# Layer-norm statistics of a gMLP gate moved from VectorE to ScalarE and GpSimd, with two changes of buffers beside them

## The chip, the cores and the metric

The kernel runs on one core of a Trainium2 chip. The metric is the time of one execution on the device, in microseconds (us); the lower the better. A core has a matrix engine (TensorE, PE in the profile; PEld is its weight load), VectorE (DVE), ScalarE (ACT), GpSimd (POOL) and SyncE (SP, which only issues transfers). Each runs its own instructions strictly in order and waits on semaphores for the others. TensorE writes to PSUM, eight banks of 128 x 512 floats; the other engines work from SBUF.

## The reference

The input x is 2048 rows of 512. It is normalised per row (xn) and goes two ways: a sliding attention (32 heads of 16, 8 taps two rows apart) with an output projection, and a gated MLP whose gate mixes the rows.

```python
xn = _layernorm(x)
s = attention(xn, wqkv) @ wo
z = gelu(xn @ w_in)                      # 2048 x 1792
z1, z2 = z[..., :896], _layernorm(z[..., 896:])
g = w_sp @ z2 + b_sp[:, None]            # w_sp is 2048 x 2048
return x + s * silu((z1 * g) @ w_out)
```

The change concerns the mean and the variance of `z2`'s rows, 896 values each: `(z - m) / sqrt(v + 1e-5)`.

## The kernel before, in words

All products are done in three passes of single-precision pieces: each operand is split into a high part (a copy on ACT, line 192) and a low part (a subtraction on DVE, line 194), and high x high, high x low and low x high are added in PSUM. So each weight needs one ACT and one DVE instruction before TensorE can use it.

The stages, in the order of TensorE's work:

1. *qkv*: the projections for attention (lines 305 and 382 to 384), until 140.8 us of the profile. Their results go to DRAM.
2. *z1* (lines 676 to 695): seven weights `w1_0` to `w1_6` of 128 columns, for each the four chunks of 512 rows, 12 matmuls a chunk, 10.9 us a weight. Each result is evicted from PSUM with a gelu on ACT (line 692; the first chunk of each weight is first scaled by DVE, line 690) and stored to DRAM.
3. *z2*, the gate (lines 697 to 778): eight pairs of row tiles (i and 8 + i, 128 rows each). Each row tile is computed in two halves of 512 and 384 columns by `z2_half` (lines 705 to 713): 12 matmuls, then a gelu from PSUM into the row tile `zt` (line 713). The weights for the halves are `w2_k_h`, four of each half.
4. *g*, the mixing by `w_sp` (line 802), written as block products over sums and differences of blocks; then the output projections *b* (lines 1044 to 1046, source `ut`) and *s* (the same lines, source the attention's output).

Attention's own arithmetic runs on DVE with low priority throughout (lines 562 to 630): products and reductions of some 2.3 us each, a first addition on POOL (line 617), and an exponential on ACT (line 592), which needs another table than gelu. Its results go through DRAM (`o_d`, line 631) and are needed by *s*.

The loop of stage 3 runs as a pipeline over three turns. In turn i the halves of pair i are computed; the statistics of pair i - 1 are taken (`z2_stats`, line 718); pair i - 2 is normalised (`z2_normal`, line 729) and its blocks combined (`combine`, line 736) and partly stored (`t_d`, lines 750 and 751). In the statistics DVE does two `bn_stats` and one `bn_aggr` a row tile (lines 722 and 723). POOL then makes from mean and variance what the normalisation needs, -m * r and r = (v + eps)^-0.5, each one number a row, in four operations (lines 724 to 727). ACT normalises with these as bias and scale (line 731).

Three sets of buffers matter.

- *Weight slots.* `weight_pair` gives out eight pairs of tiles in turn (`slot`). A weight that takes a slot waits until the last matmul with that slot's former weight. In order of calls they go to 12 weights of qkv, to `w1_0` to `w1_6`, to the four left halves `w2_k_0` and the four right halves `w2_k_1`; so `w2_0_1` to `w2_3_1` take the slots of `w1_3` to `w1_6`. The first weight of stage 4, `wsp_0_0`, has an own pair of tiles with the tags `wh` and `wl` (line 753); a bias (line 954) takes them later. `w_1h` in the profile is the high part of a `w2_k_1`, with numbers left out as in all names; a weight of z1 is `w_0h` to `w_6h` at lines 683 to 685.
- *`t4` tiles*: eight buffers of 128 x 1024, shared by z1's evictions (`z1t`), by the block sums (`sa`, `sb`), by the gate's row tiles `zt` and by a bias that stays for long (`b_a`).
- *PSUM banks*: taken in turn, so that TensorE can be eight halves (two pairs) ahead of ACT's evictions.

`block_sums` (line 388) loads four blocks of `w_sp` (SP), adds them up in four additions (DVE, line 390) and stores the sums to DRAM (POOL, line 400). There are eight such sets for stage 2: set 0 before its first weight, set f + 1 behind weight f.

Instructions are put in order on each engine by a scheduler that works with a model of their times and the priority of program order; a few are pinned to program order (fetches, splits). So a change of a few instructions can move others about. The order is fixed before the kernel runs.

Of the kernel before, what the change touches and what calls it, by code (L numbers as in the profile page):

```python
# [23 lines left out]
KB = D // P  # L24
FB = FH // P
NG = 3
CT = 512
# [17 lines left out]
EPS = 1e-5  # L45
# [12 lines left out]
def kernel(  # L58
# [13 lines left out]
    nc = tc.nc  # L72
# [36 lines left out]
    mone = const.tile([P, 9], F32, name="mone")[:, :1]  # L109
    nc.vector.memset(mone, -1.0)  # L110
    mvx = const.tile([P, NT, 2], F32, name="mvx")
    nc.vector.memset(mvx, 0.0)
    mvz = const.tile([P, NT, 2], F32, name="mvz")
    nmz = const.tile([P, NT], F32, name="nmz")

    BIG = whole.tile([P, NT * 2 * FH + 32], F32R, name="BIG")[:, 32:]
# [6 lines left out]
    def z2_at(j):  # L123
        return planes[:, :, j, 0], planes[:, :, j, 1]
# [19 lines left out]
    def blocks(t, n=KB):  # L144
        return t.rearrange("p (k q) -> p k q", k=n)
# [14 lines left out]
    def weight_pair(name):  # L160
        i = next(slot)
        return (
            wts.tile([P, 512], F32R, tag=f"whi{i}", name=name + "h"),
            wts.tile([P, 512], F32R, tag=f"wlo{i}", name=name + "l"),
        )
# [3 lines left out]
        pin(nc.sync.dma_start(raw[:, :n], src))  # L169
        return raw  # L170

    def prep(src, n, name, raw=None):
        if raw is None:
            raw = fetch(src, n, name)
        hi, lo = weight_pair(name)
        split(hi[:, :n], lo[:, :n], raw[:, :n])
        return hi, lo

# [34 lines left out]
    def late_rstd(j):  # L213
        return mvx[:, j, 1:2] if j < JC else 1.0
# [201 lines left out]
    z1_sums = [(0, i) for i in range(HT)]  # L416
# [254 lines left out]
    def first_sums(a, i):  # L671
        block_sums(a, i, stores=nc.gpsimd)

    first_sums(*z1_sums[0])

    for f in range(FB):
        wh, wl = prep(w_in1[:, f, :], KB * P, f"w1_{f}")
        for c in range(NC):
            pz = mm(f"z1_{f}_{c}")
            for k in range(KB):  # L680
                cc = slice(k * P, (k + 1) * P)
                xh, xl = [planes[:, FB - KB + k, c * JC : (c + 1) * JC, a] for a in range(2)]
# [9 lines left out]
            nc.scalar.activation(zt, pz, AF.Gelu_apprx_tanh)  # L692
# [12 lines left out]
    def z2_half(j, h, zt):  # L705
        xh, xl = xn_at(j)
        pz = mm(f"z2_{j}_{h}")[:, : WID[h]]
        for k in range(KB):
            wh, wl = [w[:, : WID[h]] for w in w2[k, h]]
            nc.tensor.matmul(pz, xh[:, k], wh, start=k == 0, stop=False)  # L710
            nc.tensor.matmul(pz, xh[:, k], wl, start=False, stop=False)  # L711
            nc.tensor.matmul(pz, xl[:, k], wh, start=False, stop=k == KB - 1)  # L712
        nc.scalar.activation(zt[:, HALF[h]], pz, AF.Gelu_apprx_tanh, scale=late_rstd(j))  # L713

    def spatial_block(c, js):
        return prep(w_sp[c, js], CT, f"wsp_{c}_{js}")

    def z2_stats(j, zt):
        st = const.tile([P, 2, 6], F32, tag="st2", name=f"zst_{j}", bufs=3)
        mv, nm = mvz[:, j], nmz[:, j : j + 1]  # L720
        for h in range(2):
            nc.vector.bn_stats(st[:, h], zt[:, h * FQ : (h + 1) * FQ])
        nc.vector.bn_aggr(mv, st)
        nc.gpsimd.tensor_tensor(nm, mv[:, 0:1], mone, op=ALU.mult)
        nc.gpsimd.tensor_scalar(mv[:, 1:2], mv[:, 1:2], EPS, None, op0=ALU.add)
        nc.gpsimd.tensor_tensor(mv[:, 1:2], mv[:, 1:2], nhalf, op=ALU.pow)
        nc.gpsimd.tensor_tensor(nm, nm, mv[:, 1:2], op=ALU.mult)  # L727

    def z2_normal(j, zt, n):
        zh, zl = z2_at(j)  # L730
        nc.scalar.activation(zt, zt, AF.Identity, bias=nmz[:, j : j + 1], scale=mvz[:, j, 1:2])  # L731
# [21 lines left out]
    early_pair = [wts.tile([P, CT], F32R, tag=f"w{n}", name=f"wsp_0_0{n}") for n in "hl"]  # L753
    split(*early_pair, fetch(w_sp[0, 0], CT, "wsp_0_0"))
    spatial = {(0, 0): early_pair}
    b_a = t4("b_a")
# [58 lines left out]
    for n in range(8):  # L815
        a, f = n // 2 % 2, n // 4 * 2 + n % 2
# [333 lines left out]
```

## Time and profile before

| | us |
|---|---|
| median of three runs | 705.97 |
| lowest and highest | 704.80, 706.61 |
| the profiled execution | 707.69 |
| its span, first to last instruction | 705.9 |
| busy in the span: PE, DVE, ACT, POOL | 691.4, 611.1, 280.6, 241.5 |

The profiled execution took 1.8 us more than its span, and 1.7 more than the median of the runs. Times in the profile count from the start of the span. In a row of a timeline stand the start, the duration, engine, line, operation and the tiles written and read; in brackets, where there was any, the time that the engine sat idle before it and what it waited for. In a row of groups, "x16 | 17.9, 1134 | 15.9 <-POOL ..." means sixteen instructions, 17.9 us busy, 1134 ns each, and 15.9 us idle before them, which POOL ended. The granted clock is the share of its full clock that TensorE got.

### The profile page before, as it was taken

How to read it: one execution, taken by the hardware profiler on the slowest of the kernel's cores; microseconds unless marked ns; L12 is line 12 of the kernel's file. 1: busy time of each engine (PE TensorE's matmuls, PEld its weight loads, DVE VectorE, ACT ScalarE, POOL GpSimd, SP SyncE). 2: the span in 40 equal slices, each digit the busy share in tenths (PEclk: the TensorE clock that was granted, in tenths of full speed). 3: DMA queues.
4: the chain of work that ended last, by engine and by line, in shares of the span. 5: the costliest groups of instructions: out<-in, count | busy, mean ns of one | idle time of the engine just before them, and what ended most of it. 6: DMA issues, size and time to landing. Idle time of an engine off the chain costs nothing.

```text
span 705.9 us, 9274 instructions
## 1 busy us (share of the span) xinstructions
PE 691.4 (98%) x3084; PEld 577.3 (82%) x3084; DVE 611.1 (87%) x878; ACT 280.6 (40%) x456; POOL 241.5 (34%) x282
## 2 busy tenths in 40 slices
PE   8999999999997999799999999999999999999997
PEld 7888888888885999688888888888888888888886
DVE  6774387898999999888998999999999999997554
ACT  4343332322424443786443454432443453221530
POOL 3105495932333376632122311223112103541500
PEclk9999999999999899899999999999999999999999
DMA  8769999779999765347799687856848775456894
GB/s 288 242 193 343 328 371 358 241 227 370 350 378 399 297 231 176 120 140 242 240 301 399 201 300 241 265 196 226 278 124 301 252 243 178 127 166 205 262 351 184
DMA packets 102080, 182.37 MB, mean 258 GB/s; under 512 B 9168, under 2 KB 45264, under 8 KB 102032
## 3 DMA queue, kind: packets, MB, share of 16 engines
q1 hardware_dynamic: 56480, 102.14, 43.3%
q0 software_dynamic: 13824, 52.24, 20.7%
q10 hardware_dynamic: 31728, 27.40, 11.6%
q8 instruction: 24, 0.39, 0.2%
q14 instruction: 24, 0.20, 0.1%
HBM read 122.42 MB, written 59.32 MB: 257 GB/s over the span
## 4 chain that ended last, share of the span: by engine, by line
PE 76%; DVE 8%; DMA 7%; issue 4%; POOL 2%; ACT 1%; SPq 1%; DVEq 0%; ACTq 0%; POOLq 0%
PE g L802 39%; PE qkv L382 5%; PE qkv L384 5%; PE qkv L383 5%; DMA sb<-in_w_sp 4%; PE b L1044 4%; PE b L1045 4%; PE b L1046 4%; PE s L1046 2%; PE s L1044 2%; PE s L1045 2%; DVE lg L569 2%; PE qkv L305 1%; DVE pr L562 1%; POOL nmz L727 1%
## 5 line engine op out<-in xcount | busy, mean ns | idle before, releaser
L617 POOL TENSOR_TENSOR pv<-pv 128x1024 f32<-128x1024 f32 x29 | 69.6, 2399 | 78.9 <-DVE pv L606 78.9
L562 DVE TENSOR_TENSOR pr<-k,q 128x2048 f32<-128x2048 f32 x32 | 75.3, 2353 | 8.6 <-DMA k<-qkv_d 4.7
L606 DVE TENSOR_TENSOR pv<-v,lg 128x2048 f32<-128x2048 f32 x32 | 73.3, 2289 | 1.4 <-DMA v<-qkv_d 0.7
L569 DVE TENSOR_REDUCE lg<-pr 128x128 f32<-128x2048 f32 x32 | 73.0, 2280 | 0.1
L631 POOL DMA_DIRECT2D o_d<-tt x32 | 18.1, 565 | 152.4 <-DVE tt L630 152.3
L430 ACT ACTIVATE stage<-qkv 128x512 f32<-128x512 f32 x36 | 21.4, 595 | 50.8 <-PE qkv L384 45.7
L710 PE MATMUL z<-w_0h,BIG 128*128 128x512 f32 x64 | 26.5, 414 | 3.7 <-ACT zt L713 3.7
L622 DVE TENSOR_TENSOR pv<-pv 128x512 f32<-128x512 f32 x32 | 24.0, 750 | 4.4 <-POOL pv L617 4.3
L1055 ACT ACTIVATE bt<-b 128x512 f32<-128x512 f32 x16 | 9.4, 597 | 43.9 <-PE b L1046 43.9
L711 PE MATMUL z<-w_0l,BIG 128*128 128x512 f32 x64 | 26.1, 408 | 0.0
L712 PE MATMUL z<-w_0h,BIG 128*128 128x512 f32 x64 | 26.0, 407 | 0.0
L1099 DVE TENSOR_TENSOR sg<-s,sg 128x512 f32<-128x512 f32 (+1 forms) x17 | 11.2, 659 | 16.9 <-PE s L1046 16.9
L711 PE MATMUL z<-w_1l,BIG 128*128 128x384 f32 x64 | 22.6, 353 | 2.8 <-DVE w_1l L194 2.8
L784 POOL DMA_DIRECT2D ol<-o_d x32 | 17.8, 556 | 20.7 <-DMA o_d<-tt 8.1
L541 POOL DMA_DIRECT2D k<-qkv_d x13 | 7.3, 560 | 50.4 <-DVE pr L562 50.4
L710 PE MATMUL z<-w_1h,BIG 128*128 128x384 f32 x64 | 22.4, 350 | 1.9 <-ACT w_1h L192 1.9
L731 ACT ACTIVATE zt<-zt,nmz,mvz 128x896 f32<-128x896 f32 x16 | 17.9, 1134 | 15.9 <-POOL nmz L727 15.9
L277 DVE TENSOR_TENSOR xT<-xT,mr 128x512 f32<-128x512 f32 x20 | 13.8, 688 | 10.9 <-DMA mr<-mv_d 6.5
L712 PE MATMUL z<-w_1h,BIG 128*128 128x384 f32 x64 | 22.5, 351 | 0.0
L194 DVE TENSOR_TENSOR BIG<-zt,BIG 128x512 fp32r<-128x512 f32 (+2 forms) x24 | 18.4, 771 | 3.7 <-ACT BIG L192 3.7
L802 PE MATMUL g<-ws_3h,BIG 128*128 128x512 f32 x52 | 20.3, 390 | 0.0
L802 PE MATMUL g<-ws_5h,BIG 128*128 128x512 f32 x52 | 20.3, 390 | 0.0
(477 smaller groups left out, 2326.7 us busy)
## 6 DMA issues: line engine op xcount, KB each, us to landing
qkv_d<-stage ACTq DMA_DIRECT2D x24, 512.0 KB
v<-qkv_d POOLq DMA_DIRECT2D x14, 704.0 KB, 4.9
k<-qkv_d POOLq DMA_DIRECT2D x13, 704.0 KB, 6.6
sums_d<-sa POOLq DMA_DIRECT2D x14, 512.0 KB, 6.6
sums_d<-sb POOLq DMA_DIRECT2D x14, 512.0 KB, 9.1
z_d<-z1t ACTq DMA_DIRECT2D x14, 512.0 KB
zl<-z_d SPq DMA_DIRECT2D x12, 512.0 KB
tr<-t_d SPq DMA_DIRECT2D x12, 384.0 KB
```

The source lines that it names most:

```text
L382: nc.tensor.matmul(pq, xh[:, k], wh, start=k == 0, stop=False)
L562: line(nc.vector.tensor_tensor(pr, taps(ks[u], j0), qb.unsqueeze(1).to_broadcast([P, W, NJ * CS]), op=ALU.mult))
L569: line(nc.vector.tensor_reduce(lgs[u][:, :, j0 * HS : (j0 + NJ) * HS], pr.rearrange("p w (i d) -> p w i d", d=DH), axis=AX.X, op=ALU.add,))
L606: line(nc.vector.tensor_tensor(pv.rearrange("p w (i d) -> p w i d", d=DH), taps(vs[u], j0).rearrange("p w (i d) -> p w i d", d=DH), lgs[u] ...
L617: eng.tensor_tensor(pv[:, 0:4], pv[:, 0:4], pv[:, 4:8], op=ALU.add)
L710: nc.tensor.matmul(pz, xh[:, k], wh, start=k == 0, stop=False)
L711: nc.tensor.matmul(pz, xh[:, k], wl, start=False, stop=False)
L712: nc.tensor.matmul(pz, xl[:, k], wh, start=False, stop=k == KB - 1)
L802: nc.tensor.matmul(pg, z[a], w[b], start=start and i == 0, stop=stop and i == 2, skip_group_check=seeded)
L1044: nc.tensor.matmul(pp[:, cols], hi, wh, start=k == 0, stop=False)
L1045: nc.tensor.matmul(pp[:, cols], hi, wl, start=False, stop=False)
L1046: nc.tensor.matmul(pp[:, cols], lo, wh, start=False, stop=k == n - 1)
```

## The change

It has three parts.

1. *Own tiles for the last weight of z1.* `w1_6` no longer takes a slot of the eight; it gets the pair tagged `wh` and `wl`, which `wsp_0_0` takes after it. All later weights move up by one slot.
2. *Two sets of block sums in front of z1*: sets 0 and 7 before the first weight, and nothing behind the last.
3. *The statistics.* Each gelu of the gate also gives the sum of its outputs (`accum_out`), one number a row. POOL makes -mean of the two sums. ACT then squares the row tile with that as bias, writes the squares to where the high part will stand later (they are not used) and gives their sum. POOL makes the variance plus eps, its power and the product. The two `bn_stats` and the `bn_aggr` on DVE go.

```diff
+    def side_pair(name):
+        return [wts.tile([P, CT], F32R, tag=f"w{n}", name=name + n) for n in "hl"]
-    def prep(src, n, name, raw=None):
+    def prep(src, n, name, raw=None, pair_=None):
...
-        hi, lo = weight_pair(name)
+        hi, lo = pair_ or weight_pair(name)
...
     first_sums(*z1_sums[0])
+    first_sums(*z1_sums[FB])
     for f in range(FB):
-        wh, wl = prep(w_in1[:, f, :], KB * P, f"w1_{f}")
+        pair_ = side_pair("w1_last") if f == FB - 1 else None
+        wh, wl = prep(w_in1[:, f, :], KB * P, f"w1_{f}", pair_=pair_)
...
-        first_sums(*z1_sums[f + 1])
+        if f < FB - 1:
+            first_sums(*z1_sums[f + 1])
...
-        nc.scalar.activation(zt[:, HALF[h]], pz, AF.Gelu_apprx_tanh, scale=late_rstd(j))
+        nc.scalar.activation(
+            zt[:, HALF[h]], pz, AF.Gelu_apprx_tanh, scale=late_rstd(j), accum_out=zsum(j, h)
+        )
+    def zsum(j, n):
+        return sums_z[:, 3 * j + n : 3 * j + n + 1]
...
     def z2_stats(j, zt):
-        st = const.tile([P, 2, 6], F32, tag="st2", name=f"zst_{j}", bufs=3)
-        mv, nm = mvz[:, j], nmz[:, j : j + 1]
-        for h in range(2):
-            nc.vector.bn_stats(st[:, h], zt[:, h * FQ : (h + 1) * FQ])
-        nc.vector.bn_aggr(mv, st)
-        nc.gpsimd.tensor_tensor(nm, mv[:, 0:1], mone, op=ALU.mult)
-        nc.gpsimd.tensor_scalar(mv[:, 1:2], mv[:, 1:2], EPS, None, op0=ALU.add)
-        nc.gpsimd.tensor_tensor(mv[:, 1:2], mv[:, 1:2], nhalf, op=ALU.pow)
-        nc.gpsimd.tensor_tensor(nm, nm, mv[:, 1:2], op=ALU.mult)
+        rstd, nm = mvz[:, j : j + 1], nmz[:, j : j + 1]
+        nc.gpsimd.tensor_scalar(
+            nm, zsum(j, 0), zsum(j, 1), -1.0 / FH, op0=ALU.add, op1=ALU.mult
+        )
+        nc.scalar.activation(
+            z2_at(j)[0], blocks(zt, FB), AF.Square, bias=nm, accum_out=zsum(j, 2)
+        )
+        nc.gpsimd.tensor_scalar(rstd, zsum(j, 2), 1.0 / FH, EPS, op0=ALU.mult, op1=ALU.add)
+        nc.gpsimd.tensor_tensor(rstd, rstd, nhalf, op=ALU.pow)
+        nc.gpsimd.tensor_scalar(nm, nm, rstd, None, op0=ALU.mult)
```

Besides, `early_pair` is made by `side_pair`, the constant `mone` goes, `mvz` keeps one number a row tile in place of two, and `sums_z` holds three.

More of the change, by code (lines that the diff above doesn't have):

```diff
@@ L108 @@
     nc.vector.memset(nhalf, -0.5)
-    mone = const.tile([P, 9], F32, name="mone")[:, :1]
-    nc.vector.memset(mone, -1.0)
     mvx = const.tile([P, NT, 2], F32, name="mvx")
     nc.vector.memset(mvx, 0.0)
-    mvz = const.tile([P, NT, 2], F32, name="mvz")
+    mvz = const.tile([P, NT], F32, name="mvz")
+    sums_z = const.tile([P, 3 * NT], F32, name="sums_z")
     nmz = const.tile([P, NT], F32, name="nmz")
@@ L718, in z2_stats @@
     def z2_stats(j, zt):
-        st = const.tile([P, 2, 6], F32, tag="st2", name=f"zst_{j}", bufs=3)
-        mv, nm = mvz[:, j], nmz[:, j : j + 1]
-        for h in range(2):
-            nc.vector.bn_stats(st[:, h], zt[:, h * FQ : (h + 1) * FQ])
-        nc.vector.bn_aggr(mv, st)
-        nc.gpsimd.tensor_tensor(nm, mv[:, 0:1], mone, op=ALU.mult)
-        nc.gpsimd.tensor_scalar(mv[:, 1:2], mv[:, 1:2], EPS, None, op0=ALU.add)
-        nc.gpsimd.tensor_tensor(mv[:, 1:2], mv[:, 1:2], nhalf, op=ALU.pow)
-        nc.gpsimd.tensor_tensor(nm, nm, mv[:, 1:2], op=ALU.mult)
+        rstd, nm = mvz[:, j : j + 1], nmz[:, j : j + 1]
[8 more added lines that the diff above has]
+        nc.gpsimd.tensor_scalar(nm, nm, rstd, None, op0=ALU.mult)
     def z2_normal(j, zt, n):
         zh, zl = z2_at(j)
-        nc.scalar.activation(zt, zt, AF.Identity, bias=nmz[:, j : j + 1], scale=mvz[:, j, 1:2])
+        nc.scalar.activation(zt, zt, AF.Identity, bias=nmz[:, j : j + 1], scale=mvz[:, j : j + 1])
         split(zh[:, :n], zl[:, :n], blocks(zt, FB)[:, :n])
@@ L751, in combine @@
         nc.sync.dma_start(t_d[2, i], b21)
-    early_pair = [wts.tile([P, CT], F32R, tag=f"w{n}", name=f"wsp_0_0{n}") for n in "hl"]
+    early_pair = side_pair("wsp_0_0")
     split(*early_pair, fetch(w_sp[0, 0], CT, "wsp_0_0"))
```

## The prediction

> **What bounds the kernel now.** I read the page's busy shares first, then TensorE's waits, then the stretches around them.
>
> ```profile
> PE 691.4 (98%) x3084; PEld 577.3 (82%) x3084; DVE 611.1 (87%) x878; ACT 280.6 (40%) x456; POOL 241.5 (34%) x282
> ```
>
> TensorE sets the end: whatever doesn't give it back idle time gives nothing. So the next view is who it waited for (total, times, longest, in us):
>
> ```profile
> PE z L710 <- ACT zt L713: 3.7, 1, 3.7
> PE z L711 <- DVE w_1l L194: 2.8, 1, 2.8
> PE z L710 <- ACT w_1h L192: 1.9, 1, 1.9
> ```
>
> All three lie in one stage, the gate's half of the projection (lines 705 to 713). The stretches (length, then PE, PEld, DVE, ACT and POOL busy, granted clock, DMA share, GB/s) show what they cost:
>
> ```profile
> 216.73:222.20 5.47, 5.47 (x26) 4.54 (x25) 5.47 (x5) 3.00 (x6) 2.48 (x2) 1.00 1.04 406
> 222.20:236.00 13.80, 9.12 (x35) 8.12 (x34) 13.60 (x23) 4.43 (x7) 6.16 (x8) 0.75 1.03 396
> 236.00:282.50 46.50, 46.50 (x233) 41.78 (x231) 45.63 (x77) 20.31 (x30) 28.42 (x37) 1.00 0.60 209
> 282.50:295.00 12.50, 8.79 (x27) 6.92 (x27) 10.95 (x24) 8.35 (x15) 6.54 (x13) 0.73 0.36 113
> 295.00:308.60 13.60, 13.60 (x72) 12.62 (x71) 10.59 (x23) 11.22 (x18) 6.09 (x15) 1.00 0.36 134
> 308.60:330.40 21.80, 21.77 (x96) 17.64 (x96) 19.46 (x28) 15.37 (x27) 9.39 (x16) 1.00 0.58 186
> ```
>
> Each stop takes the granted clock down with it (0.75 and 0.73), so its price is idle time plus slow matmuls. TensorE's timeline gives both; the first and last row bound the stage:
>
> ```profile
> 216.95 0.39 PE L710 MATMUL z<-w_0h,BIG 128*128 128x512 f32 x1
> ...
> 223.80 0.34 PE L712 MATMUL z<-w_1h,BIG 128*128 128x384 f32 x1
> ...
> 234.34 0.40 PE L711 MATMUL z<-w_0l,BIG 128*128 128x512 f32 x1
> ...
> 294.75 0.33 PE L710 MATMUL z<-w_1h,BIG 128*128 128x384 f32 x1
> 298.94 0.39 PE L710 MATMUL z<-w_0h,BIG 128*128 128x512 f32 x1
> ...
> 304.42 0.33 PE L710 MATMUL z<-w_1h,BIG 128*128 128x384 f32 x1
> 308.60 0.39 PE L802 MATMUL g<-wsp_0h,BIG 128*128 128x512 f32 x1
> ```
>
> From 298.94 to 308.60 an undisturbed pair of row tiles takes 9.66: 24 matmuls of 512 columns (0.228 apart) and 24 of 384 (0.174 apart). Eight pairs are 77.3; the stage took 308.60 - 216.95 = 91.65, so 14.35 is lost. The first stop: between 223.80 and 234.34 lie 16 steps of 384 and one of 512, worth 3.0, in 10.5: 7.5 lost. The second has the rest, 6.85, of which 3.7 is idle, so some 3 is slow clock. After 308.60 TensorE is full (21.77 of 21.80): what is gained here arrives at the end, if nothing later is late.
>
> **Part 1: own tiles for the last weight.** The 8 weight slots go round. Before, the last right-half weight takes the slot of w1_6, which is read until 216.95:
>
> ```profile
> 225.43 0.52 ACT L192 ACTIVATE w_1h<-w_1r 128x384 fp32r<-128x384 f32 x1
> 228.66 0.55 DVE L194 TENSOR_TENSOR w_1l<-w_1r,w_1h 128x384 fp32r<-128x384 f32 x1
> ```
>
> The high part comes 8.5 after the slot is free, the low part 11.7. After, w1_6 has its own pair, every later weight moves one slot forward, and the last takes the slot of w1_5, free one weight (48 matmuls of 0.227 = 10.9) earlier. With the same lags the low part ends at 228.66 + 0.55 - 10.9 = 218.3; TensorE wants it at 224.0. The stop goes: **-7.5**. The pair is shared with wsp_0_0, whose split now waits for w1_6 to be read out; its reader is L802, from 308.60, which hides that. The fetch and split counts are unchanged.
>
> **Part 2: block sums moved forward.** Set 7 was issued behind the last z1 weight; now it stands before the first. Its two loads on SP, four additions on DVE and two stores on POOL are not removed, they leave this stage:
>
> ```profile
> 258.04 0.64 DVE L390 TENSOR_TENSOR sb<-sa,sb 128x512 f32<-128x512 f32 x1
> L713 ACT ACTIVATE zt<-z,mvx 128x512 f32<-128x512 f32 x4 | 2.7, 683 | 9.5 <-DMA sums_d<-sa 7.2 <-PE z L712 2.3
> ```
>
> The first gate eviction waited 7.2 for a sums store: the sums hold the t4 buffers that the gate's rows need, and set 7 still added at 258. With it gone seven buffers (the bias has one) serve three and a half pairs from the start. In front, set 7 stands where set 1 was, with as many loads and additions, so I take 0. If its four additions (4 x 0.64 = 2.6) came on top before a z1 eviction, and that emptied TensorE's lead, the cost would be up to 2.6 plus the 3 of slow clock; nothing there argues for a gain.
>
> **Part 3: the statistics.** Off DVE go these:
>
> ```profile
> L722 DVE BATCH_NORM_STATS2 zst<-zt 128x6 f32<-128x448 f32 x32 | 18.4, 609 | 0.0
> L723 DVE BATCH_NORM_AGGREGATE mvz<-zst 128x2 f32<-128x12 f32 x16 | 3.0, 192 | 0.0
> ```
>
> 21.4 leaves DVE. To ACT come 16 squares over 128x896 and 48 sums read out (32 evictions, 16 squares). The nearest rows:
>
> ```profile
> L731 ACT ACTIVATE zt<-zt,nmz,mvz 128x896 f32<-128x896 f32 x16 | 17.9, 1134 | 15.9 <-POOL nmz L727 15.9
> L192 ACT ACTIVATE BIG<-zt 128x896 fp32r<-128x896 f32 x8 | 7.6, 948 | 0.1
> L713 ACT ACTIVATE zt<-z 128x512 f32<-128x512 f32 x12 | 7.1, 588 | 0.0
> L713 ACT ACTIVATE zt<-z 128x384 f32<-128x384 f32 x12 | 5.8, 487 | 1.0 <-PE z L712 1.0
> ```
>
> A square has one per-row operand: between the copy without (0.948) and the normalisation with two (1.134), 1.04; x16 = 16.7. No row shows a read-out of the sum: at least 0, at most a whole 384-column activation (0.487, x48 = 23.4). I take the line through 384 and 512 columns at no columns, 0.588 - 4 x 0.101 = 0.18; x48 = 8.6. ACT was busy 3.00 + 4.43 + 20.31 + 8.35 + 11.22 = 47.3 in the stage, so it needs 72.6, against 77.3 for TensorE. ACT's last gate eviction may end some 2.5 after TensorE's stage (an estimate: five evictions of 0.5), so 79.8 - 72.6 = 7.2 of waiting is free. **That is the crux**, because ACT is in order and the normalisation now waits twice for POOL: sum, square, variance, power, product.
>
> ```profile
> L727 POOL TENSOR_TENSOR nmz<-nmz,mvz 128x1 f32<-128x1 f32 x16 | 14.9, 934 | 0.7
> L724 POOL TENSOR_TENSOR nmz<-mvz,mone 128x1 f32<-128x1 f32 x16 | 7.1, 446 | 16.9 <-DVE mvz L723 16.7
> 278.58 5.68 POOL L727 TENSOR_TENSOR nmz<-nmz,mvz 128x1 f32<-128x1 f32 x1
> 284.13 0.19 DVE L723 BATCH_NORM_AGGREGATE mvz<-zst 128x2 f32<-128x12 f32 x1
> 284.29 1.13 ACT L731 ACTIVATE zt<-zt,nmz,mvz 128x896 f32<-128x896 f32 x1 [4.61 <-POOL nmz L727]
> ```
>
> This is the cause of the second stop. A 128x1 product took 5.68 and ended as DVE reached an operation with one tensor input; ACT sat 4.61, the evictions behind it came late, TensorE ran out of banks. POOL in turn idled 16.7 for DVE's statistics, which stand behind attention work. So of ACT's 15.9 I put half, 8, to DVE's lateness, which goes, and half to POOL's own held operations, which stay. POOL has four small operations a row before and after; their cost is between nothing changed and one more such hold (5.7) per pair, and I take nothing, as the extra hop of one pair lies beside the next pair's evictions. With 8 of waiting, 0.8 over the free 7.2, one short stop remains: 0.8 + 3 of slow clock = 3.8. Of the 6.85 some **3.0** is won.
>
> In the trace, the second stop's row ends as DVE comes to its statistics. The Trainium skill (SBUF — State Buffer, Who interferes with whom) says that a DVE instruction with two SBUF inputs and a reading GpSimd instruction hold each other off entirely, and one with at most one input doesn't. By that the change removes the very instructions that let POOL in, and the sum would be that of the first rival.
>
> **What follows later.** Attention ends on DVE shortly before the last projection uses it:
>
> ```profile
> 658.11 0.39 PE L1044 MATMUL s<-BIG 128*128 128x512 f32 x1
> 661.83 0.69 DVE L194 TENSOR_TENSOR o_3l<-ol,o_3h 128x512 fp32r<-128x512 f32 x1
> ```
>
> The first group of rows takes 4 x 12 matmuls of 0.227 = 10.9, so the second group's low part (662.5) is wanted from 669: 6.5 spare. A stage that ends 10.5 earlier needs attention 4 earlier; DVE loses 21.4 and was full, so this holds. With no DVE time reaching it the gain would shrink by 4.
>
> **Sum.** -7.5 - 3.0 = -10.5 on the profiled execution: 707.69 - 10.5 = 697.2. That execution is 1.7 over the median of the three runs, 705.97; on the median, **695.5**.
>
> **The rivals.**
> 1. *ACT paces the stage (slower).* Place: the two POOL hops of each row. If each hop waits as today's one does (2 x 15.9), ACT needs 72.6 + 31.8 = 104.4, 24.6 over the free 79.8, against 14.35 lost today: +10.3, 716. It decides from 72.6 + w = 79.8 + 14.35, w = 21.5. For it: the 5.68 row, and denser two-input work on DVE. Against: half the wait was DVE's. Near w = 21.5 it is no change.
> 2. *Only the first stop goes*: -7.5, 698.5, if ACT's waits stay near today's size at one place.
> 3. *The first stop stays*, the change not doing what it says: ACT's in-order queue holds the weight's split whatever slot is free. -3.0, 703. Against: 5.7 of slack.
> 4. *Attention late at the last projection*: -6.5, 699.5.
> 5. *The square needs another function table than the gelu.* A load took 1.28:
>
> ```profile
> L592 ACT ACT_TABLE_LOAD x3 | 3.8, 1283 | 0.5 <-ACT z1t L692 0.4
> ```
>
> Two per pair for 8 pairs are 20.5 more on ACT: 72.6 + 20.5 + 8 - 79.8 = 21.3 lost, +7, 713. No normalisation or copy today brings a load. The Trainium skill (ScalarE: Activation LUTs, Table sets) names cheap functions that are in every set, the square not among them; no run here shows it.
>
> **How the numbers follow.** Forecast (both stops go, up to 6 left; 691 to 698) 0.42. Rival 1: slower 0.24, within 0.3% 0.07. Rival 2 0.14, rival 3 0.04, rival 4 0.05, rival 5 0.04. So faster 0.42 + 0.14 + 0.04 + 0.05 = 0.65, same 0.07, slower 0.28; 0.3% (2.1 us) is about what a measurement of this kernel tells from no change. Low end: all 14.35 won and a run like the lowest of the three, 690.5. At the top, the slower cases spread from 708 to 725 with the read-out's upper end; leaving out the worst 0.2 of them gives 711.
>
> **What would show it.** Part 1: TensorE's wait for w_1l is gone, and the last such copy on ACT is before 220. Part 2: no DVE addition of sa or sb after 245, and no ACT wait for sums_d. Part 3: the stage takes about 81 from first gate matmul to first L802; ACT's waits for POOL there sum to under 10; a square lasts 1.04 and the read-out 0.18. I am wrong if ACT's busy time plus its waits in the stage pass 90, if TensorE stops at a new place (a z1 eviction, the last projection), or if table loads multiply.

## The result and the profile after

The changed kernel takes 713.75 us (median of 4 runs) against 706.29 for the kernel before beside it: ratio 1.0099, 95% interval 1.0073 to 1.0126, so slower by 0.7 to 1.3%. The profiled execution's span is 713.0, against 705.9. Line numbers below are those of the kernel named; in the changed one the first projection is L687 to 697, the gate L715 to 742, the first g stage L813.

The page's busy shares and TensorE's waits in the changed kernel:

```profile
PE 691.9 (97%) x3084; PEld 576.4 (81%) x3084; DVE 596.7 (84%) x829; ACT 302.1 (42%) x522; POOL 244.7 (34%) x282
```

```profile
PE z L687 <- DVE z1t L694: 6.5, 1, 6.5
PE g L813 <- ACT wsp_1h L194: 5.2, 1, 5.2
PE g L813 <- ACT g L831: 2.9, 1, 2.9
```

None of the three waits of before is left, and three new ones stand at other places: one in the first projection (z, L687), two at the start of g. The stretches (length, PE, PEld, DVE, ACT, POOL busy, granted clock, DMA share, GB/s):

```profile
227.60:304.60 77.00, 77.00 (x384) 69.11 (x382) 68.00 (x95) 53.52 (x109) 48.32 (x64) 1.00 0.61 222
304.60:324.00 19.40, 11.28 (x36) 8.38 (x36) 13.60 (x17) 19.16 (x39) 6.99 (x11) 0.74 0.27 86
sum 96.40, PE 88.28 PEld 77.48 DVE 81.60 ACT 72.68 POOL 55.31; mean PE 44.14 PEld 38.74 DVE 40.80 ACT 36.34 POOL 27.66
```

The gate is clean: 77.0 of 77.0 busy with all its 384 matmuls. Right behind it TensorE has 11.28 of 19.40, while ACT is full (19.16 of 19.40). The first new stop, on TensorE's timeline (start, duration):

```profile
174.04 0.39 PE L689 MATMUL z<-BIG,w_2l 128*128 128x512 f32 x1
180.97 0.80 PE L687 MATMUL z<-BIG,w_3h 128*128 128x512 f32 x1 [6.54 <-DVE z1t L694]
181.57 0.63 PE L688 MATMUL z<-BIG,w_3h 128*128 128x512 f32 x1
```

After 6.5 us of idle time the matmuls start 0.4 to 0.6 apart instead of 0.23. The table below has this ledger for every kernel: "first projection" from its first matmul to the gate's, "gate" from its first to the end of its last matmul, "lag" from there to the start of ACT's last gate eviction (ACT reads TensorE's PSUM bank directly and so frees it), "rest" from that same end of the gate to the end of the span. These columns come from one profiled execution, which can lie some us from the median (p13_g_dve: 718.7 against 714.13); each ratio is against runs of the kernel before beside it. What the later kernels hold is told with their experiments. As an example the two rows that give 18.8 for the changed kernel (323.53 less 304.43 + 0.34):

```profile
304.43 0.34 PE L717 MATMUL z<-w_1h,BIG 128*128 128x384 f32 x1
```

```profile
323.53 0.49 ACT L718 ACTIVATE zt<-z 128x384 f32<-128x384 f32 x1
```

| kernel (what it holds) | first projection | gate | lag | rest | span | median, ratio [95% interval] |
|---|---|---|---|---|---|---|
| before | 76.2 | 91.8 | 2.3 | 397.1 | 705.9 | 706.29 beside the changed kernel |
| changed (parts 1, 2, 3) | 85.6 | 77.5 | 18.8 | 408.2 | 713.0 | 713.75, 1.0099 [1.0073, 1.0126] |
| p1_own_tiles (1) | 76.2 | 85.2 | 12.1 | 407.3 | 709.8 | 710.55, 1.0055 [1.0032, 1.0078] |
| p2_sums_front (2) | 83.4 | 77.4 | 8.4 | 398.5 | 700.6 | 703.13, 0.9949 [0.9920, 0.9978] |
| p3_stats (3) | 76.2 | 82.8 | 14.8 | 406.9 | 708.3 | 709.41, 1.0024 [1.0003, 1.0045] |
| p13_no_front (1, 3) | 76.2 | 81.1 | 14.2 | 407.3 | 706.3 | 709.73, 1.0036 [1.0010, 1.0062] |
| p12_no_stats (1, 2) | 85.5 | 77.6 | 5.2 | 401.2 | 705.4 | 705.94, 0.9986 [0.9962, 1.0011] |
| p2_two (2, at most two sets) | 76.2 | 82.9 | 9.5 | 405.5 | 706.2 | 710.83, 1.0080 [1.0045, 1.0116] |
| p12_two (1, 2, at most two sets) | 76.2 | 79.0 | 21.0 | 408.6 | 704.9 | 704.34, 0.9970 [0.9939, 1.0001] |
| late7 (set 7 late in the gate) | 76.2 | 81.5 | 10.6 | 413.0 | 711.9 | 714.37, 1.0121 [1.0068, 1.0174] |
| late7_p1 (the same, and 1) | 76.2 | 78.4 | 19.0 | 415.5 | 711.2 | 712.94, 1.0092 [1.0057, 1.0126] |
| after_half (changed, half the statistics on DVE) | 86.3 | 77.6 | 15.7 | 408.0 | 712.7 | 714.83, 1.0142 [1.0103, 1.0181] |
| after_g_dve (changed, first results for g on DVE) | 82.8 | 77.7 | 19.9 | 415.4 | 717.5 | 719.33, 1.0168 [1.0124, 1.0213] |
| after_two_g_dve (the same, at most two sets) | 76.2 | 83.1 | 16.0 | 406.0 | 706.2 | 707.81, 1.0015 [0.9988, 1.0042] |
| p13_g_dve (1, 3, first results for g on DVE) | 78.5 | 86.1 | 16.6 | 411.3 | 716.9 | 714.13, 1.0108 [1.0055, 1.0160] |
| after_no_square (changed, no squares) | 81.7 | 78.1 | 21.7 | 420.9 | 725.8 | 726.49, 1.0254 [1.0224, 1.0284] |
| after_no_pool (changed, ACT never waits for POOL) | 82.8 | 77.6 | 4.4 | 396.9 | 698.9 | 700.70, 0.9902 [0.9867, 0.9936] |
| after_pow (changed, three POOL operations on DVE) | 82.7 | 77.6 | 5.9 | 400.6 | 703.0 | 705.86, 0.9983 [0.9959, 1.0007] |
| p2_pow (2, the same) | 85.0 | 78.0 | 21.9 | 408.7 | 713.4 | 714.38, 1.0093 [1.0057, 1.0130] |
| p12_two_pow (1, 2, at most two sets, the same) | 76.2 | 82.9 | 20.0 | 407.3 | 707.7 | 710.42, 1.0049 [1.0023, 1.0074] |

Against before, the changed kernel wins 14.3 in the gate and loses 9.4 in the first projection, 11.1 in the rest, and 0.8 as the first projection starts later: +7.0, the span's +7.1. Gate and lag together, the time from TensorE's first gate matmul to the start of ACT's last eviction, are 94.1 before and 96.3 in the changed kernel: the stage got 14.3 shorter for TensorE and not for ACT.

### The profile page after: what moved, and what is told of

The parts are those of the page before. It is cut to its first block, busy times and chain, and to the rows that moved or that the text cites. A ratio compares the mean times of both kernels' runs of the same rounds, so it can differ in the third digit from the quotient of the medians.

```text
span 713.0 us, 9299 instructions
## 1 busy us (share of the span) xinstructions
PE 691.9 (97%) x3084; PEld 576.4 (81%) x3084; DVE 596.7 (84%) x829; ACT 302.1 (42%) x522; POOL 244.7 (34%) x282
## 3 DMA queue, kind: packets, MB, share of 16 engines
q10 hardware_dynamic: 31728, 27.40, 11.3%
## 4 chain that ended last, share of the span: by engine, by line
PE 62%; DVE 13%; DMA 9%; ACT 5%; POOL 5%; issue 4%; SPq 1%; DVEq 0%; POOLq 0%; ACTq 0%
PE g L813 38%; PE b L1056 4%; PE b L1057 4%; PE b L1055 4%; DMA sb<-in_w_sp 3%; PE s L1056 2%; PE s L1057 2%; PE s L1055 2%; DVE pr L564 2%; DVE lg L571 2%; DMA w_1r<-in_w_in 1%; PE qkv L386 1%; PE qkv L385 1%; PE qkv L307 1%; PE qkv L384 1%
## 5 line engine op out<-in xcount | busy, mean ns | idle before, releaser
L795 POOL DMA_DIRECT2D ol<-o_d x32 | 17.7, 555 | 42.9 <-DVE o_1l L196 14.8
L196 DVE TENSOR_TENSOR BIG<-zt,BIG 128x512 fp32r<-128x512 f32 (+2 forms) x24 | 18.9, 796 | 12.1 <-ACT BIG L194 12.0
L717 PE MATMUL z<-w_0h,BIG 128*128 128x512 f32 x64 | 25.1, 392 | 0.0
L715 PE MATMUL z<-w_0h,BIG 128*128 128x512 f32 x64 | 24.9, 389 | 0.0
L279 DVE TENSOR_TENSOR xT<-xT,mr 128x512 f32<-128x512 f32 x20 | 13.7, 687 | 12.1 <-DMA mr<-mv_d 7.2
L717 PE MATMUL z<-w_1h,BIG 128*128 128x384 f32 x64 | 21.5, 336 | 0.0
L715 PE MATMUL z<-w_1h,BIG 128*128 128x384 f32 x64 | 21.5, 336 | 0.0
L716 PE MATMUL z<-w_1l,BIG 128*128 128x384 f32 x64 | 21.5, 335 | 0.0
L696 ACT ACTIVATE z1t<-z 128x512 f32<-128x512 f32 x21 | 12.0, 592 | 21.9 <-DMA z_d<-z1t 19.1
L813 PE MATMUL g<-ws_1h,BIG 128*128 128x512 f32 x52 | 20.3, 390 | 0.0
```

Of the source, the lines that this page charges most:

```text
L813: nc.tensor.matmul(pg, z[a], w[b], start=start and i == 0, stop=stop and i == 2, skip_group_check=seeded)
```

## The experiments

**Each part by itself, and two of them.** Three kernels hold one part of the diff each, one holds parts 1 and 3, and a later one parts 1 and 2.

> Part 1 alone on the kernel before. Theory A (each stop has one part as its cause): the first gate stop (7.5 us with its slow clock) goes, because the last right-half weight takes a slot that is free 10.9 us earlier; the second gate stop (6.85) stays; no stop in z1 and none at the start of g. Time 7 to 8 us under before, some 698.5. Theory B (the stops are an accident of the order that the scheduler makes anew at every change): the first stop goes, but another of a few us comes at some other place, and the time is within 3 us of before.

> Part 2 alone on the kernel before. Theory A: the stop in z1 comes with it, at the fourth weight, 6.5 us idle and 3 of slow clock; the first gate stop stays (7.5), the second is smaller or gone, because the gate's first eviction no longer waits for a sums store. Time 9.6 us over before if the second stop stays, 3 over if it goes: 709 to 716. Theory B: no stop in z1, as it needs the order that part 1 or part 3 brings; time within 4 us of before.

> Part 3 alone on the kernel before. Theory A: no stop in z1; the first gate stop stays (7.5); the second goes; TensorE stops at the start of g for ACT, by less than the 11.6 us of the changed kernel, because the first gate stop gives ACT 7.5 us more: 0 to 6. Time between 7 us under and 2 over before, 699 to 708. Theory C (ACT has room; the stop at the start of g is the late start of ACT that the z1 stop left behind): no stop at g at all, 6 to 7 us under before.

> The changed kernel without part 2 (sets of block sums as before). Theory A: no stop in z1, both gate stops gone, the stop at g stays at 8 us idle or more, since ACT has the squares and the sums in addition: 9 to 10 us under the changed kernel, some 704. Theory C (ACT is late at g only because z1 ended badly): the stop at g goes too: 20 us under the changed kernel, some 693. Theory B: stops at other places, any time.

The table's rows follow each part. *Own tiles* shorten the gate by 6.6, but the rest grows by 10.2: the wait for w_1l is gone, and TensorE stops 6.1 for an eviction in the gate and 3.2 for one at the start of g. *Block sums in front* alone bring the stop into the first projection (+7.2) and still win: the gate is clean and the rest nearly as before. *The statistics* shorten the gate by 9.0 and lengthen the rest by 9.8. So the stop of z comes from part 2 alone, and the stop at g needs no part 2: part 3 alone waits there, and the kernel of parts 1 and 3 too, for each its longest wait (p3_stats, then p13_no_front).

```profile
PE g L811 <- ACT wsp_1h L194: 7.2, 1, 7.2
```

```profile
PE g L811 <- ACT wsp_1h L194: 7.1, 1, 7.1
```

All four times miss theory A's forecasts. Part 1 alone got its new stop, as theory B had it, and is 3.4 us slower than before. Parts 3, and 1 and 3, stop at g somewhat as theory A had it (7.2 and 7.1, where it said at most 6 and at least 8), but what they win in the gate doesn't reach the end. Part 2 alone is faster than any theory said, because the wait for the last weight is gone without own tiles. p2_two below, which differs in having no stop in z, waits 1.5 for that weight's low part again; so the stop in z is what gave the weight time.

**Never more than two sets of block sums at a time.** After the sets 0 and 7 in front:

```
-        if f < FB - 1:
-            first_sums(*z1_sums[f + 1])
+        for n in ((), (1,), (2,), (3,), (4,), (5, 6), ())[f]:
+            first_sums(*z1_sums[n])
```

late7 leaves set 7 out of the loop and puts it behind turn 5 of the gate (`raw_sums(0, HT - 1)`); late7_p1 adds the own tiles.

> Part 2 alone, but with sets 0 and 7 in front, none behind the first weight, and then sets 1 to 4 behind weights 1 to 4, sets 5 and 6 behind weight 5; so two sets of sums are loaded at the start of z1 as before, not three. Theory A (three sets at once take all eight t4 tiles, and VectorE stands for their late loads): the z1 stop (4.5 us idle, 7.2 with the slow clock) goes, the gate stage stays clean at 77.3; 7 us under part 2 alone, some 696. Theory E (any additional set in z1 overloads its transfers): a stop of 3 us or more stays somewhere in z1, and the time is within 3 us of part 2 alone.

> The kernel before with set 7 of the block sums neither in front nor behind the last z1 weight, but in turn 5 of the gate stage with raw tiles in place of t4 tiles. Theory A (the second gate stop comes from the t4 tiles that set 7 holds at the start of the gate stage): the second gate stop goes, no stop in z1; the first stop, the late weight, stays (7.5) as nothing but part 1 or a delayed z1 mends it: 6 to 7 us under before, some 699 to 700. Theory F (set 7's place has nothing to do with it): the second stop stays, time within 3 us of before.

> The same with part 1, the own tiles for the last z1 weight. Theory A: both gate stops gone, no stop in z1, none at g because ScalarE has no squares: z2 in 77.3, 13 to 15 us under before, 692 to 694. Theory B (stops are accidents of the order): one of several us at a new place, as in the run of part 1 alone; time 697 or more.

> Own tiles and block sums in front without the new statistics, and never more than two sets of block sums at a time. The stop in the first projection (6.6 us of idle time with three sets at once) goes: its stage takes 76.2 us. What TensorE wins there is kept only if ScalarE and VectorE are not late at the start of g: if they are not, 696 to 700, the best kernel; if the win only moves the wait to the gate and to g, as it did with the block sums alone (710.8 against 703.1), 704 to 711. I hold the second for likelier.

In all four, as in after_two_g_dve and p12_two_pow below, the first projection takes 76.2. With three sets at once it took 81.7 to 86.3 in every kernel. (p13_g_dve, with one set in front, has 78.5: a later wait of 1.6.) So three sets at once are the cause, shown by taking away one; they hold six of the eight t4 tiles, not all eight as the expectation has it. SyncE's queue in the changed kernel shows them: six loads (sa, sb) of 512 KB within 4 us, where the kernel before has four there.

```profile
155.64 0.38 SPq L397 DMA_DIRECT2D sa<-in_w_sp  x1
156.07 0.46 SPq L397 DMA_DIRECT2D sb<-in_w_sp  x1
156.58 0.46 SPq L397 DMA_DIRECT2D sa<-in_w_sp  x1
157.09 0.47 SPq L397 DMA_DIRECT2D sb<-in_w_sp  x1
157.66 0.55 SPq L168 DMA_DIRECT2D w_1r<-in_w_in  x1
158.25 0.54 SPq L397 DMA_DIRECT2D sa<-in_w_sp  x1
158.84 0.88 SPq L397 DMA_DIRECT2D sb<-in_w_sp  x1
```

Two things then hold the evictions of z, as DVE's and ACT's timelines show:

```profile
169.05 0.69 DVE L392 TENSOR_TENSOR sa<-sa 128x512 f32<-128x512 f32 x1
176.80 0.69 DVE L392 TENSOR_TENSOR sb<-sa,sb 128x512 f32<-128x512 f32 x1 [7.06 <-DMA sb<-in_w_sp]
...
180.29 0.63 DVE L694 TENSOR_TENSOR z1t<-z,rb 128x512 f32<-128x512 f32 x1
```

```profile
171.64 0.60 ACT L696 ACTIVATE z1t<-z 128x512 f32<-128x512 f32 x1 [8.74 <-DMA z_d<-z1t]
176.60 0.60 ACT L696 ACTIVATE z1t<-z 128x512 f32<-128x512 f32 x1 [4.36 <-DMA z_d<-z1t]
```

DVE stands 7.06 at an addition whose load is still on its way, and the scaling of z (L694) that TensorE's bank waits for is queued behind it. ACT waits for a store of z1t to give back one of the eight t4 tiles, six of which hold sums. Which of the two costs more was not tried.

In none of these kernels is the won time kept whole. p2_two has 7.2 less in the first projection than p2_sums_front, 5.5 more in the gate and 7.0 more in the rest. p12_two's rest is 7.4 longer than that of p12_no_stats, and its lag 21.0. p12_two, at 704.34, came out where the likelier of its two forecasts put it. For the other three theory A's times were more than 14 us too low: late7's and late7_p1's gates are 10.3 and 13.4 shorter than before (about 7 and 14 were forecast), but their rests are 15.9 and 18.4 longer. The reading that fits is that the delay of TensorE in the first projection gave ACT and DVE time to catch up; it is argued from the table, not tried by itself. The lag isn't the new statistics' alone either: p12_two and late7_p1 have the old ones, and lags of 21.0 and 19.0.

**Why TensorE stops at g: order, load, or waits of ACT.** First, half of the row tiles' statistics were given back to DVE (`on_act(j)` is `j < HT`):

> The changed kernel, with the statistics of row tiles 8 to 15 by VectorE as before and only those of 0 to 7 by ScalarE. It takes 8 squares (1.04 us), 24 read-outs (0.19) off ScalarE, some 13 us of the stage. Theory A (ScalarE's load makes the stop at the start of g): that stop, 8.1 us idle and 3 of slow clock, goes or falls under 2; the z1 stop stays; 10 to 11 us under the changed kernel, 702 to 704. Theory D (not the load, but the place of the first g weight's split in ScalarE's order): the stop stays at 5 us idle or more, and the time within 4 us of the changed kernel.

The stop stays (7.0 and 1.9 idle), and the lag with it (15.7): ACT has less to do and waits longer. Its longest waits for POOL in the gate (total, times, longest; with a third, 2.9, they are 23.8 against 10.6 in the changed kernel):

```profile
ACT zt L759 <- POOL nmz L755: 11.9, 4, 6.4
ACT BIG L750 <- POOL nmz L747: 9.0, 5, 3.6
```

The numbers are those of theory D, the place in ACT's order, which the next kernels try. DVE took the high parts of weights 1 to 3 and the seeds of g, the results that TensorE had waited for; weights 2 and 3 are also prepared earlier, beside weight 1 in the last gate turn:

```
+        if on_dve:
+            first_ = pin(nc.vector.tensor_copy(hi, src))
...
-                    spatial[0, 1] = spatial_block(0, 1)
+                    for js in range(1, 4):
+                        spatial[0, js] = spatial_block(0, js)
...
-            seed(0, f, biases[0][0])
+            nc.vector.tensor_copy(banks[0, f], biases[0][0])
```

> The changed kernel with the high parts of the first g stage's weights 1 to 3 and its four bias seeds made by VectorE instead of ScalarE. In the changed kernel ScalarE's last gate eviction starts 18.8 us behind TensorE's last gate matmul (2.4 in the kernel before) and TensorE loses 11.6 us at the start of g, waiting for ScalarE's seed (2.9) and weight split (5.2), which stand behind 26 to 29 of the 32 gate evictions in ScalarE's queue. Theory Q (only the place in ScalarE's queue counts): both waits go, at most 2 of the 11.6 us stay, the time is 703 to 706. Theory L (ScalarE's load counts: it is 18.8 us behind, whatever stands where in its queue): TensorE meets the next late ScalarE result, a normalised row of the gate, within 30 us after the start of g, and stops there about as long; the time stays at 711 to 714. The stop in the first projection stays in both (6 to 7.5 us of idle time).

> The same with the block sums never more than two sets at a time (0 and 7 in front, 1 to 4 behind weights 1 to 4, 5 and 6 behind weight 5). Both theories: the stop in the first projection goes (its stage takes 76.2 instead of 85.6 us). Theory Q: the 9.5 us arrive at the end, 694 to 697, the best kernel so far. Theory L: TensorE reaches g earlier and waits there longer for ScalarE; 703 to 711, and the wait at g is 3 to 9 us longer than in the kernel above.

> Own tiles and the new statistics without the block sums in front (709.7 us, ratio 1.0036, with a wait of 7.1 us for ScalarE's weight split at the start of g), with the high parts of weights 1 to 3 and the four seeds made by VectorE. Theory Q: the 7.1 us go, with some 2.5 of slow clock, 700 to 702. Theory L: a row of the gate is late instead, 707 to 710.

> The changed kernel without the new statistics (own tiles and block sums in front). If the statistics cost what ScalarE's lag says, the lag at the end of the gate is near the 8.4 us of the block sums alone, the loss at g is 1 to 4 us, the stop in the first projection stays at 4.5 to 7 us, and the time is 702 to 706: so the changed kernel's last loss is the statistics' own. If the new order of the weights makes the wait at g, it stays near 5 us without the statistics and the time is 710 to 714.

TensorE's waits in after_g_dve:

```profile
PE g L819 <- DVE wsp_1h L197: 5.4, 1, 5.4
PE g L819 <- ACT BIG L199: 4.7, 1, 4.7
...
PE g L819 <- DVE g L968: 3.1, 1, 3.1
```

That only the place in ACT's queue counts fell at once. The same two waits are there, now for DVE, as long as before; and a gate row's high part (BIG) is late in addition, as theory L had it. DVE's timeline shows what stands ahead of the weight: low parts of the gate's rows, for which DVE waits for ACT's high parts.

```profile
303.88 0.56 DVE L201 TENSOR_TENSOR BIG<-zt,BIG 128x384 fp32r<-128x384 f32 x1 [2.08 <-ACT BIG L199]
...
311.04 0.42 DVE L197 CAST wsp_1h<-wsp_1r 128x512 fp32r<-128x512 f32 x1
```

ACT's lateness counts, wherever TensorE meets it. The times of after_g_dve (719.33) and p13_g_dve (714.13) are above both theories' forecasts, that of after_two_g_dve (707.81) is in theory L's. Without the statistics (p12_no_stats) the lag is 5.2 and the time that of before: added to parts 1 and 2, part 3 costs the whole step from a ratio of 0.9986 to 1.0099.

Then what makes ACT late, its added work or its waits for POOL? One kernel leaves out the squares, so no variance enters its rows; the other lets squares and normalisations take a constant, so neither mean nor variance does. The second one's edit:

```
-            z2_at(j)[0], blocks(zt, FB), AF.Square, bias=nm, accum_out=zsum(j, 2)
+            z2_at(j)[0], blocks(zt, FB), AF.Square, bias=nhalf, accum_out=zsum(j, 2)
...
-        nc.scalar.activation(zt, zt, AF.Identity, bias=nmz[:, j : j + 1], scale=mvz[:, j : j + 1])
+        nc.scalar.activation(zt, zt, AF.Identity, bias=nhalf, scale=nhalf)
```

> The changed kernel without its 16 squares and their read-outs (16.6 + 3.0 us of ScalarE's time); GpSimd's variance operation reads an eviction's sum instead, so GpSimd has as many operations as in the changed kernel, and the variance is wrong. Theory W1 (ScalarE's own added work makes it 18.8 us late at the end of the gate): the lag falls by some 15 to 20 us, the 11.6 us at the start of g fall to 0 to 3, the time is 702 to 706. Theory W2 (the waits for GpSimd behind GpSimd's held operations make it late): the waits grow where the work goes, as with half of the rows given back to VectorE (lag 15.7, 714.8 us); the lag stays above 12 and the time is 709 to 714. The stop in the first projection stays in both, 6 to 7.5 us.

> The changed kernel with all its operations, but the squares and the normalisations take a constant in place of GpSimd's mean and factor, so ScalarE waits for GpSimd nowhere in the gate; the rows come out wrong. ScalarE waited 12.4 us for GpSimd in this stage. Theory W1: the lag stays above 10 us, the loss at g at 6 to 11 us, the time is 709 to 714. Theory W2: the lag falls to 3 to 8 us, the loss at g to 0 to 3 and the time to 702 to 706. If work and waits simply add up in ScalarE's queue, both this kernel (18.8 - 12.4 = 6.4) and the one without squares come out between 702 and 707.

With all of ACT's work and no wait for POOL the lag is 4.4, g starts without a stop, and the time is 700.7, in spite of the stop in the first projection. Of the 14.1 that its span is shorter, 11.3 are in the rest, behind the gate; 2.8 are in the first projection, whose stop is shorter though the edit doesn't touch it, so another order of the instructions has a part in the total. ACT's groups in the gate of that kernel (count, busy, mean ns, idle before):

```profile
L742 ACT ACTIVATE zt<-zt,nhalf 128x896 f32<-128x896 f32 x16 | 18.1, 1138 | 0.1
L733 ACT ACTIVATE BIG<-zt,nhalf 128x896 fp32r<-128x896 f32 x16 | 16.7, 1043 | 0.2
```

Without the squares ACT has 19.6 less to do, but its waits at the one hop to POOL that is left grow from 10.6 for both hops to 27.5, and the lag to 21.7; TensorE stops 10.2 at g. Why these waits grow so far isn't shown. ACT's wait first, then TensorE's:

```profile
ACT zt L739 <- POOL nmz L735: 27.5, 12, 4.1
```

```profile
PE g L810 <- ACT wsp_1h L194: 10.2, 1, 10.2
```

So the waits make the changed kernel's lag, not the added work, and the two don't simply add up. In the changed kernel ACT's waits for POOL between 227 and 324 are 10.6 in all (the 12.4 of the expectation counts later ones too); taking them away shortened the lag by 14.4, of which 2.6 come from a first eviction that starts 11.5 into the stage in place of 14.1.

```profile
ACT zt L742 <- POOL nmz L738: 5.9, 6, 1.6
ACT BIG L733 <- POOL nmz L730: 4.7, 4, 2.1
```

**Three of POOL's four operations on DVE.** Only the power stays; the edit for the changed kernel:

```
-        nc.gpsimd.tensor_scalar(
+        nc.vector.tensor_scalar(
             nm, zsum(j, 0), zsum(j, 1), -1.0 / FH, op0=ALU.add, op1=ALU.mult
         )
...
-        nc.gpsimd.tensor_scalar(rstd, zsum(j, 2), 1.0 / FH, EPS, op0=ALU.mult, op1=ALU.add)
+        nc.vector.tensor_scalar(rstd, zsum(j, 2), 1.0 / FH, EPS, op0=ALU.mult, op1=ALU.add)
         nc.gpsimd.tensor_tensor(rstd, rstd, nhalf, op=ALU.pow)
-        nc.gpsimd.tensor_scalar(nm, nm, rstd, None, op0=ALU.mult)
+        nc.vector.tensor_scalar(nm, nm, rstd, None, op0=ALU.mult)
```

> The changed kernel with three of GpSimd's four small operations per row made by VectorE; only the power stays on GpSimd. Without any wait for GpSimd's results the changed kernel's lag was 4.4 us instead of 18.8 and the time 700.7. Theory H (GpSimd's operations are held while VectorE works, each for up to some us, and the four together make the waits): the waits for a row's statistics fall below 8 us, the lag below 10, the time is 703 to 708. Theory V (any engine that also does the attention's long operations hands the row on as late: VectorE's queue takes the place of the hold): ScalarE waits 12 us or more for VectorE and GpSimd together, the lag stays above 14, the time is 711 to 716.

> Block sums in front alone (703.1 us), with three of GpSimd's four small operations per row as two of VectorE. ScalarE waited 21.1 us for GpSimd's last operation there. Theory H: these waits fall by half and more; as the stage and g lose only 1.3 us there, the time gains at most 1 to 2: 701 to 703. Theory V: waits as before, 703 to 706.

> Own tiles, block sums in front and never more than two sets at a time, old statistics (704.3 us, first projection clean, ScalarE 21 us late at the end of the gate and waiting 21.5 us for GpSimd), with the same three operations on VectorE. Theory H: the waits fall by half and more, the lag at the end below 10, the stops at the gate and at g (some 7 us of idle time) go: 696 to 700, the best kernel. Theory V: 702 to 707.

On the changed kernel the lag falls from 18.8 to 5.9, the stop at g goes, and the time with it: 705.86, the time of before, as theory H forecast. Again 3.0 of the 10.0 that the span is shorter are in the first projection, which the edit doesn't touch. What the operations last shows in the groups, the changed kernel's first, then this one's:

```profile
L730 POOL TENSOR_SCALAR nmz<-sums_z 128x1 f32<-128x1 f32 x15 | 10.9, 728 | 17.8 <-ACT zt L718 17.7
L737 POOL TENSOR_TENSOR mvz<-mvz,nhalf 128x1 f32<-128x1 f32 x14 | 10.9, 778 | 1.1
```

```profile
L737 POOL TENSOR_TENSOR mvz<-mvz,nhalf 128x1 f32<-128x1 f32 x15 | 19.7, 1316 | 30.7 <-DVE mvz L736 30.6
L730 DVE TENSOR_SCALAR nmz<-sums_z 128x1 f32<-128x1 f32 x16 | 3.2, 207 | 0.3 <-ACT zt L718 0.3
```

The mean takes 0.21 on DVE where it took 0.73 on POOL; the power that stays has a longer mean (1.32 against 0.78), for which two rows of 5.54 and 3.61 are enough. On the other two bases the same step failed: the waits for POOL went, and others came. p2_pow (714.38) and p12_two_pow (710.42) are slower than both theories said. In p2_pow ACT waits for DVE:

```profile
ACT zt L732 <- DVE nmz L728: 15.1, 5, 3.9
ACT BIG L192 <- DVE zt L745: 11.9, 2, 7.9
```

There DVE still makes the statistics proper. In p12_two_pow ACT waits 20.5 for DVE and 22.6 for stores. So neither theory of the expectations holds for all three: with the statistics' bulk on ACT, fewer operations on POOL help; with it on DVE, DVE's queue and stores take the place of the waits for POOL. What part the order of the instructions has in p2_pow, whose stop comes later (6.6, at L962 for an eviction), stays open.

The fastest version with the reference's rows is p2_sums_front, part 2 alone: 703.13, ratio 0.9949.

## Why the prediction was wrong

Forecast were 695.5 and a range of 690.5 to 711; measured 713.75.

- **What bounds the kernel:** the stage, its loss of 14.35 and both causes were right: the changed kernel has the gate clean (77.0 of 77.0), even the residual of 3.8 is gone. The step "after 308.60 TensorE is full: what is gained here arrives at the end" failed. It carried the condition "if nothing later is late" and checked it for attention only. In the trace of before, ACT's last eviction starts 2.3 behind TensorE's gate, after TensorE had twice stopped for ACT or DVE. That ACT would still be so near without these stops was assumed; from TensorE's first gate matmul on it took 94.1 before and 96.3 after, where the sum gave it 79.8, and the lag of 18.8 is paid at the start of g, where the rest grows by 11.1.
- **Part 1, -7.5:** the mechanism was right, no wait for w_1l is left with the own tiles. Alone the gate gains 6.6 and the rest loses 10.2, for which the sum had no term.
- **Part 2, taken as 0, at most 5.6:** measured 9.4 with the whole change and 7.2 alone. "Set 7 stands where set 1 was" was the error: set 1 did not leave. Three sets are loaded at once, which takes six of eight t4 tiles and puts DVE's wait for a load ahead of a z eviction. Counting loads and additions missed what they hold. Yet part 2 alone, for which the sum saw no argument for a gain, is the one part that is faster: its stop in z spares the two in the gate.
- **Part 3:** the sizes of the work were right. A square was to last 1.04 and a read-out 0.18; measured:

```profile
L733 ACT ACTIVATE BIG<-zt,nmz 128x896 fp32r<-128x896 f32 x16 | 16.6, 1040 | 4.9 <-POOL nmz L730 4.7
L718 ACT ACTIVATION_READ_ACCUMULATOR zt<-z 128x1 f32 x24 | 4.7, 195 | 0.0
```

  ACT's need was to be 72.6; between 227.6 and 324.0, from the gate's start to ACT's last eviction, it was busy 72.68, some of g's first work among it, so that the two agree to 0.1 is partly chance. The waits are what failed: the sum gave ACT 79.8 for work and waits, it took 96.4. Of the 23.7 idle, 10.6 are for POOL, where 8 were taken, and most of the rest comes before the first eviction, which waits for a z1 store to free a t4 tile and starts 14.1 into the stage:

```profile
241.37 0.69 ACT L718 ACTIVATE zt<-z,mvx 128x512 f32<-128x512 f32 x1 [6.58 <-DMA z_d<-z1t]
```

  The sum had no start: it counted ACT's time from the stage's first matmul, though in the trace of before the first eviction starts 16.7 into the stage, behind the wait for set 7's store that part 2 was to end. That wait did end, and one for a z1 store stood in its place. Before:

```profile
233.68 1.16 ACT L713 ACTIVATE zt<-z,mvx 128x512 f32<-128x512 f32 x2 [7.25 <-DMA sums_d<-sa]
```

  The last eviction, put 2.5 behind the stage, came 18.8 behind it. Two of the prediction's own signs of being wrong came: ACT's busy time and waits passed 90, and TensorE stopped for a z1 eviction.
- **Rival 1** had the right place, the two POOL hops of each row, and the right sign, at 716. Its price was laid to the gate, and its deciding point (21.5 us of waiting) was not reached: the waits for POOL in the gate were 10.6. TensorE's eight banks, worth two pairs or 19.3 us, can cover the lag of 18.8 in the stage; it is paid where g needs ACT's next results. Rivals 2, 3 and 5 didn't happen: both gate stops went, and between 227 and 324 ACT has four table loads, not two per pair, two for attention's exponential (L594) and two back to the gelu (L718), none at a square:

```profile
L594 ACT ACT_TABLE_LOAD x2 | 2.6, 1283 | 0.0
L718 ACT ACT_TABLE_LOAD x2 | 2.6, 1283 | 0.0
```

- **Attention late at the end (rival 4):** no wait of TensorE for the last projection's weights is among the changed kernel's longest.
- **POOL's held operations:** in the changed kernel the same operation (L730) lasts 1.38 beside DVE's two-input work and 0.26 in a gap of DVE between 296.76 and 297.94. POOL's rows, then DVE's:

```profile
286.53 1.38 POOL L730 TENSOR_SCALAR nmz<-sums_z 128x1 f32<-128x1 f32 x1 [1.73 <-ACT zt L718]
...
297.15 0.26 POOL L730 TENSOR_SCALAR nmz<-sums_z 128x1 f32<-128x1 f32 x1 [2.79 <-ACT zt L718]
```

```profile
284.98 2.27 DVE L564 TENSOR_TENSOR pr<-k,q 128x2048 f32<-128x2048 f32 x1
287.18 0.67 DVE L624 TENSOR_TENSOR pv<-pv 128x512 f32<-128x512 f32 x1
...
296.21 0.55 DVE L755 TENSOR_TENSOR zt<-zt,zt 128x384 f32<-128x384 f32 x1
297.94 1.09 DVE L196 TENSOR_TENSOR BIG<-zt,BIG 128x896 fp32r<-128x896 f32 x1 [1.18 <-ACT BIG L194]
```

  The Trainium skill (SBUF — State Buffer, Who interferes with whom) says that a DVE instruction with two SBUF inputs and a reading GpSimd instruction hold each other off. The trace agrees with that rule in these rows, 1.38 against 0.26. What the prediction drew from it, that the change takes away what lets POOL in, doesn't show: the longest of the 64 row operations on POOL is 2.69 in the changed kernel and 5.68 before. That the hold alone makes ACT's waits isn't shown: p2_pow has one such operation per row and was slower.

## What to carry to other kernels

A stage that is freed of its stops hands its helper engines' lag to the next stage: before adding the gain, look how far the in-order helpers end behind the bounding engine, and count that as a term. In this stage added work on a helper with room was nearly free, round trips to another busy engine were not: with the added 26 us on ACT (16.6 of squares, 48 read-outs of some 0.19) and no wait for POOL the rest was 396.9, as before (397.1), when ACT had less to do and waited 15.9 for POOL. Moving a load forward isn't neutral because its count stays the same; ask which buffers and which in-order queue it then shares with what was already there.

## What the runs showed of the hardware

- An activation's sum costs ACT an instruction of its own: 0.19 us, for 128x1, behind the evictions as behind the squares (0.195 and 0.189 mean).
- A small operation on POOL can last very long, whether anybody waits or not, and its mean says little. In after_no_pool one power of 128x1 lasts 10.52, the other fifteen 0.57 to 2.20. From 280.21 on DVE ran sixteen instructions with two tensor inputs without a gap; the power ended at 290.75, just behind DVE's next instruction with one input. POOL's row, then DVE's:

```profile
280.23 10.52 POOL L737 TENSOR_TENSOR mvz<-mvz,nhalf 128x1 f32<-128x1 f32 x1
```

```profile
290.24 0.42 DVE L632 STREAM_TRANSPOSE tt<-pv 128x256 f32<-128x256 f32 x1
```

  DVE's busy share alone doesn't tell it: in the kernel before, with DVE 94% busy in the gate, the sixteen powers last 0.54 to 0.98.
- A stop of TensorE costs more than its idle time: 6.5 idle in the changed kernel's first projection lengthened it by 9.4, as the matmuls behind it start up to 0.6 apart, where 0.23 is usual.
